# The last pair's second product as seven block products, its squares on ScalarE, and weight sums made later

## The chip, the cores and the metric
The kernel runs on one core of one Trainium2 chip (trn2). The time is the device time of the core in microseconds (us); the median of three runs before the change is 1382.69 us (1381.63 to 1384.86).

## What is computed
Attention without a softmax, normed per head, then two MLPs on 4608 tokens of width 512, all in f32:

```python
kv = einsum('bhsd,bhse->bhde', k, v); out = einsum('bhsd,bhde->bhse', q, kv)
x = out / sqrt(mean(out * out) + 1e-06) * g_norm           # 4608 x 512 after a transpose
r = maximum(x @ w_in, 0.0); x = (s * (r * r) + b) @ w_out  # first MLP, 2048 wide
h = maximum(maximum(x @ w1, x @ w2), x @ w3)               # second MLP, 768 wide
return h @ w_out2
```

## The kernel before, in words
Tokens lie in nine tiles of 512 columns. Each f32 product is three matmuls with rounded operands: high by high, high by low, low by high, so operands are split into two parts, the high one on ScalarE and the rest on VectorE (`hilo`, line 174).

**First MLP.** `h` has 16 chunks f of 128 rows, `y` four chunks j. Tiles 0 to 2 are multiplied plainly: for each f 12 matmuls for h, then relu, square times s (`squared`, line 437), plus b and split (`gate`, line 444), then 12 matmuls into four PSUM banks of y. Tiles 3 to 8 go in three pairs (ta, tb). The first product of a pair is made in eight turns q of seven block products (`h_steps`, line 658): 2x2 blocks with the two tiles as one side and two chunks f as the other, 6 matmuls each, 42 a turn where plain products would take 48. Their operands are sums of tokens (`tok_steps`, line 609) and sums of weights, 1792 KB a turn (`wp_dr`). A turn yields four blocks: chunks 2q and 2q+1 of each tile. Those of ta are gated at once, and the second product of ta runs beside the next turn (`y_mm`, line 469, 24 matmuls as fill). Those of tb go to DRAM (`g_dr`); after the eight turns the class `Second` (line 1402) reloads them one by one, gates each two chunks ahead and runs tb's second product, 192 matmuls.

**Second MLP.** Five groups of tokens (`SUPERS`, the first is tiles 1 and 2). In each, nine units `v1` (line 724) of seven block products, 42 matmuls a unit, with maxima between the three weights, then `Output` (line 798), again seven block products over three chunks. Units take weight sums of 1792 KB from DRAM (`wc_dr`), the output three such tiles (`wo_dr`).

**Weight preparation.** The class `Ahead` (line 512) holds a list of steps, each a load and a make: `pair_op` (sums for the pairs), `plain_op` (an f64 weight chunk to f32, stored), `combine` (four differences and sums of 256 columns, a split of 768 and one of 1024 columns, a 1792 KB store). `beside_of` spreads such steps and token operands over the matmuls counted by `tick`; from the third pair on they may be moved forward freely, before that they stand behind the last main instruction (`in_order`). Order within an engine is set at compile time by a scheduler from program order and dependences; every engine runs its queue in order, and all DMAs named here are issued by the SP queue.

**Buffers.** Gates: two, and one more (`gp`, `gS`), each high and low. Weight tiles of 1792 KB: two (`wa`), a third in the second MLP (`wb`). PSUM: four banks y, two h, one x, one more; in the second MLP four o, one each of a, b, x, d.

Of the kernel before, what the change touches and what calls it, by code (L numbers as in the profile page):

```python
# [8 lines left out]

# [61 lines left out]
def fused_kernel(ctx, tc, qt, kv, kvr, g_norm, w_in, w_out, s, b, w1, w2, w3, w_out2, out):  # L71
# [55 lines left out]
    g_sb, sb_sb, rsb = cst[:, 0:1], cst[:, 1:3], cst[:, 3:4]  # L127
    kvbd2 = ap1.tile([P, NP, 2, P], F32R, tag="kvbd", name="kvbd")
# [13 lines left out]
    wo_dr = [dram.tile([P, 2, 7, HW], F32, name=f"wo_dr{c}") for c in range(KM // 2)]  # L142
# [297 lines left out]

    turn = [0]
    w2p = {}

    def gate(r):
# [5 lines left out]
        nc.scalar.activation(out=gh, in_=r, func=ACTF.Identity, bias=sb_sb[:, 1:2])  # L450
        nc.vector.scalar_tensor_tensor(out=gl, in0=r, scalar=sb_sb[:, 1:2], in1=gh.bitcast(F32), op0=ALU.add, op1=ALU.subtract)  # L451
# [27 lines left out]
    def y_out(t, o, n, j, st, acc):  # L479
        y = yt[t, o][j][:, :n]  # L480
        if acc:
            nc.vector.tensor_tensor(out=st, in0=st, in1=y, op=ALU.add)
        elif j % 2:
            nc.scalar.activation(out=st, in_=y, func=ACTF.Copy)
        else:
            nc.vector.tensor_copy(st, y)
        store(y_dr[t][:, j, o:o + n], st)
# [66 lines left out]

    def combine(srcs, tile_of, dst):

        def blocks(t):
            return t.bitcast(F32).rearrange("p (n c) -> p n c", c=HW)
# [10 lines left out]
        return load, maker(got, blocks, tile_of, dst)  # L569

    def maker(got, blocks, tile_of, dst):

        def make():
# [9 lines left out]
            hilo(tgt[:, 0, 0:3], tgt[:, 1, 0:3], raw[:, 1:4])  # L583
            hilo(tgt[:, 0, 3:7], tgt[:, 1, 3:7], com)
            store(dst, tgt.bitcast(F32), 18)
# [72 lines left out]
    def h_steps(w, T, tb, q, gates):  # L658
# [3 lines left out]
        fa, fb = 2 * q, 2 * q + 1  # L662
# [10 lines left out]

        def keep(f, r):
            store(g_dr[tb][f], r)
# [15 lines left out]
        def p2():  # L691
# [3 lines left out]
            squared(r, a)  # L695
            gates[fa] = gate(r)

        def p4():
            d, r = got.pop("d"), fpool("r")
            prod(w, T, d, A22, "t4", False, False, end)  # L700
            nc.vector.tensor_tensor(out=r, in0=d, in1=got.pop("u2"), op=ALU.add)
            squared(r, r)
            gates[fb] = gate(r)

        def p5():
            x, r = got.pop("x"), fpool("r")
            prod(w, T, x, S1, "t1", False, False, end)
            got["b"] = copy(h_bank("b"), x)
            nc.vector.tensor_tensor(out=r, in0=x, in1=got.pop("p7"), op=ALU.add)
            squared(r, r)  # L710
            keep(fb, r)

        def p3():
            b, r = got.pop("b"), fpool("r")
            prod(w, T, b, S4, "b22", False, False, end)
            squared(r, b)
            keep(fa, r)
# [658 lines left out]
    direct = {}  # L1376
# [284 lines left out]
```

## Time and profile before
| | us |
|---|---|
| median of three runs | 1382.69 |
| profiled execution, device time | 1380.73 |
| its span, first to last instruction | 1378.9 |
| TensorE busy | 1363.6 |
| VectorE busy | 967.8 |
| ScalarE busy | 735.6 |

The span is cut into stages by the matmuls of the trace: the first pair's first product from 327.5 us, its stored half from about 463; the second pair from about 510, its stored half from about 645; the third pair from 688.0, its stored half from about 808; the second MLP from 853.5. PE is TensorE, DVE VectorE, ACT ScalarE, SP the queue that issues DMAs. Busy times of one engine overlap at the ends of instructions, and busy TensorE is modelled.

### The profile page before, as it was taken

The numbers are of one execution on the slowest core, as the hardware profiler recorded it, in microseconds if no ns is written. First come the engines' busy times: TensorE is split into PE (matmuls) and PEld (weight loads), VectorE is DVE, ScalarE is ACT, GpSimd is POOL, SyncE is SP. The second block draws the span as 40 slices with busy tenths as digits, with TensorE's granted clock in tenths as the row PEclk, the third lists the DMA queues.
The fourth block names the chain that finished last, engine by engine and source line by source line (L and its number), as shares of the span: only waits on it lengthen the run. The fifth ranks groups of instructions, "written<-read, shape, count | busy, mean of one in ns | idle before, by whom it ended". The sixth has DMA issues, their size and how long they took to land.

```text
span 1378.9 us, 19476 instructions
## 1 busy us (share of the span) xinstructions
PE 1363.6 (99%) x6870; PEld 1129.6 (82%) x6870; DVE 967.8 (70%) x1768; ACT 735.6 (53%) x1420; POOL 11.0 (1%) x40
## 2 busy tenths in 40 slices
PE   8999999999999999999999999999999999999998
PEld 6878887888888888887878878888998888888886
DVE  8999866678877678777967676547674574666555
ACT  7975655566776546565555554334453452443332
POOL 1000000000000000000000000000000000000000
PEclk9999999999999999999999999999999999999999
DMA  8486544585666856779898899955864554563532
GB/s 307 141 260 210 190 138 138 183 273 198 236 241 253 315 182 212 271 243 300 296 354 298 300 323 373 395 187 167 323 219 170 211 186 153 195 240 115 178 143 62
DMA packets 144584, 316.39 MB, mean 229 GB/s; under 512 B 62438, under 2 KB 82406, under 8 KB 133734
## 3 DMA queue, kind: packets, MB, share of 16 engines
q1 hardware_dynamic: 144480, 315.15, 65.9%
q8 instruction: 54, 0.88, 0.3%
q14 instruction: 44, 0.36, 0.1%
q10 hardware_dynamic: 6, 0.00, 0.0%
HBM read 222.30 MB, written 92.80 MB: 229 GB/s over the span
## 4 chain that ended last, share of the span: by engine, by line
PE 82%; DVE 8%; DMA 5%; issue 2%; ACT 2%; SPq 0%; POOL 0%; DVEq 0%; ACTq 0%; POOLq 0%
PE x L465 18%; PE y L465 18%; PE d L465 12%; PE o L465 9%; PE a L465 6%; PE b L465 6%; PE h L423 5%; PE y L151 2%; PE h L151 2%; DVE tb L151 1%; PE ops L343 1%; PE kvps L321 1%; DMA gb<-g_dr 1%; DVE head L151 1%; DMA raw<-in_w_in 1%
## 5 line engine op out<-in xcount | busy, mean ns | idle before, releaser
L465 PE MATMUL y<-gh,w 128*128 128x512 f32 x976 | 319.0, 391 | 1.3 <-ACT gh L450 1.1
L465 PEld LDWEIGHTS y<-gh,w 128*128 128x128 f32 x976 | 182.9, 188 | 40.1 <-ACT gh L450 2.0
L465 PE MATMUL d<-t,wc 128*128 128x512 f32 (+1 forms) x828 | 199.4, 376 | 0.3 <-ACT p L734 0.3
L465 PE MATMUL x<-t,wc 128*128 128x512 f32 (+1 forms) x828 | 199.5, 376 | 0.1
L465 PE MATMUL y<-gl,w 128*128 128x512 f32 x488 | 191.1, 392 | 1.0 <-DVE gl L451 0.8
L465 PEld LDWEIGHTS d<-t,wc 128*128 128x128 f32 x828 | 148.7, 188 | 28.4 <-ACT p L734 0.5
L465 PEld LDWEIGHTS x<-t,wc 128*128 128x128 f32 x828 | 148.3, 188 | 28.0 <-ACT a L671 0.5
L739 DVE TENSOR_TENSOR c<-d,u 128x512 f32<-128x512 f32 (+1 forms) x45 | 28.7, 638 | 134.7 <-PE d L465 134.7
L439 DVE SCALAR_TENSOR_TENSOR r<-r,cst 128x512 f32<-128x512 f32 x107 | 80.0, 749 | 47.3 <-ACT r L438 46.4
L465 PEld LDWEIGHTS y<-gl,w 128*128 128x128 f32 x488 | 91.7, 188 | 20.2 <-DVE gl L451 2.7
L465 PE MATMUL a<-b,wc 128*128 128x512 f32 (+1 forms) x414 | 100.1, 376 | 0.0
L465 PE MATMUL x<-b,wc 128*128 128x512 f32 (+1 forms) x414 | 99.9, 376 | 0.0
L465 PE MATMUL b<-b,wc 128*128 128x512 f32 (+1 forms) x414 | 99.5, 376 | 0.0
L465 PEld LDWEIGHTS b<-b,wc 128*128 128x128 f32 x414 | 74.4, 188 | 14.3 <-ACT b L671 0.4
L465 PEld LDWEIGHTS x<-b,wc 128*128 128x128 f32 x414 | 74.2, 188 | 14.0 <-issue 0.4
L465 PEld LDWEIGHTS a<-b,wc 128*128 128x128 f32 x414 | 74.2, 188 | 13.8
L465 PE MATMUL o<-t,wq 128*128 128x512 f32 (+1 forms) x354 | 75.5, 369 | 0.0
L734 ACT ACTIVATE a<-x 128x512 f32<-128x512 f32 (+1 forms) x45 | 24.3, 539 | 92.9 <-PE x L465 92.9
L151 PE MATMUL h<-xh,w 128*128 128x512 f32 (+1 forms) x216 | 72.0, 377 | 0.0
L465 PEld LDWEIGHTS o<-t,wq 128*128 128x128 f32 x354 | 62.4, 188 | 11.2
L734 ACT ACTIVATE b<-x 128x512 f32<-128x512 f32 (+1 forms) x45 | 24.3, 539 | 81.2 <-PE x L465 81.2
L151 PE MATMUL y<-gh,w 128*128 128x512 f32 (+1 forms) x200 | 65.2, 371 | 1.1 <-ACT st L151 1.1
(165 smaller groups left out, 2371.9 us busy)
## 6 DMA issues: line engine op xcount, KB each, us to landing
wc<-wc_dr SPq DMA_DIRECT2D x45, 1792.0 KB, 7.4
wc<-wp_dr SPq DMA_DIRECT2D x16, 1792.0 KB, 8.4
kv<-in_kv SPq DMA_DIRECT2D x32, 512.0 KB, 5.9
wc_dr<-hl SPq DMA_DIRECT2D x9, 1792.0 KB, 9.2
gb<-g_dr SPq DMA_DIRECT2D x62, 256.0 KB, 4.7
wp_dr<-wc SPq DMA_DIRECT2D x8, 1792.0 KB, 7.5
g_dr<-r SPq DMA_DIRECT2D x51, 256.0 KB, 2.6
y_dr<-st SPq DMA_DIRECT2D x48, 256.0 KB, 3.3
```

The lines of the kernel that those rows point to most:

```text
L151: tail[eng] = call(*args, **kw).ins
L321: nc.tensor.matmul(pb[d, i * D:(i + 1) * D], lhsT=t[:, 0, d], rhs=t[:, 1, d], start=(c == 0), stop=(c == NC))
L343: nc.tensor.matmul(pb, lhsT=l, rhs=r, start=(i == 0), stop=(i == 2))
L423: nc.tensor.matmul(h[:, :n], lhsT=w[:, z, kk, :], rhs=x[:, kk, o:o + n], start=(i == 0), stop=(i == 3 * KD - 1))
L439: main["dve"] = nc.vector.scalar_tensor_tensor(out=r, in0=r, scalar=sb_sb[:, 0:1], in1=r, op0=ALU.mult, op1=ALU.mult).ins
L465: ins = nc.tensor.matmul(*args, **kw)
L734: main["act"] = nc.scalar.activation(out=out, in_=pb, func=ACTF.Copy).ins
L739: main["dve"] = nc.vector.tensor_tensor(out=o, in0=pb, in1=t, op=ALU.add).ins
```

## The change
Three parts.

1. For the last pair (tiles 7, 8) the class `Blocks` takes the place of `y_mm` and `Second`. The second product is also made in seven block products, for each of 8 chunk pairs q, with 2 output parts of 128 rows and 3 matmuls each. Two of the seven (b11, t3) run beside the next turn of the first product; the other five in a run of 40 blocks behind it, each with a gate or split of its own. Results of the first product stay in the memory of used-up weights instead of DRAM. The weights for the blocks are made from `w_out` by `block_op`, one step for each q, among the preparations of the first two pairs (8 steps), go to DRAM (`ws_dr`, `wh_dr`), and come back in chunks of 1792 KB.
2. In all pairs s times the square of the relu is made on ScalarE as the square of root(|s|) times it, and the sum and relu in front of it by one custom VectorE instruction; the sign of s is put on b and on the results of the second product. `roots` makes root and sign once.
3. The sums of the second MLP's units 3 to 8 and two of the three output weights are no longer made in the last pair but in the first group, one step behind each of units 0 to 7, into the tiles in which they are used.

```diff
+    root, sign, bias, tmp = cst[:, 4:5], cst[:, 5:6], cst[:, 6:7], cst[:, 7:9]
...
+    def roots():
+        a, e = tmp[:, 0:1], tmp[:, 1:2]
+        s_, b_ = sb_sb[:, 0:1], sb_sb[:, 1:2]
+        nc.scalar.activation(out=a, in_=s_, func=ACTF.Abs)
...
+        nc.scalar.activation(out=root, in_=a, func=ACTF.Abs_reciprocal_sqrt)
...
+    def rooted(out, src, relu):
+        if relu:
+            nc.scalar.activation(out=out, in_=src, func=ACTF.Relu)
+        main["act"] = nc.scalar.activation(out=out, in_=out if relu else src, func=ACTF.Square, scale=root).ins
+
+    def relu_sum(out, bank, t):
+        main["dve"] = nc.vector._custom_dve(TENSOR_ADD_SAT, out=out, in0=bank, in1=t, s0=3.4028235e38, s1=0.0).ins
...
+    def scaled(st, y, by_act, signed=True):
+        if by_act:
+            nc.scalar.activation(out=st, in_=y, func=ACTF.Copy, **({"scale": sign} if signed else {}))
+        elif signed:
+            nc.vector.tensor_scalar(out=st, in0=y, scalar1=sign, scalar2=None, op0=ALU.mult)
...
-            squared(r, a)
-            gates[fa] = gate(r)
+            rooted(r, a, True)
+            sink(0, 0, r)
...
-            nc.vector.tensor_tensor(out=r, in0=d, in1=got.pop("u2"), op=ALU.add)
-            squared(r, r)
-            gates[fb] = gate(r)
+            relu_sum(r, d, got.pop("u2"))
+            rooted(r, r, False)
+            sink(1, 0, r)
...
+    def block_op(q):
...
+            for i, w in enumerate((fa, fb)):
+                hi, lo = (w[:, z].bitcast(F32).rearrange("p (n c) -> p n c", c=HW) for z in range(2))
+                nc.vector.tensor_tensor(out=raw[:, 2 * i:2 * i + 2], in0=hi, in1=lo, op=ALU.add)
...
+            tt(0, raw[:, 1], raw[:, 3], ALU.add)
+            tt(1, com[:, 0], raw[:, 0], ALU.subtract)
+            tt(2, raw[:, 2], com[:, 1], ALU.subtract)
+            tt(3, raw[:, 0], raw[:, 1], ALU.subtract)
...
+                hilo(hi, lo.bitcast(F32R), lo)
+                for k in range(2):
+                    store(to[2 * i + k][:, 0], hi[:, k].bitcast(F32))
+                    store(to[2 * i + k][:, 1], lo[:, k])
...
-    prep.todo += conv[:16]
+    parts = [block_op(q) for q in range(QF)]
+    for q in range(QF):
+        prep.todo += [parts[q], conv[q]]
...
+    prep.todo += [*conv[QF:], *com[:3], outs[2]]
+    inside = Ahead()
+    inside.todo += [*com[3:], *outs[:2]]
...
+    class Blocks:
...
+        def sink(self, q):
...
+            def sink(i, j, x):
+                r[i, j] = x
+                if (i, j) == (0, 0):
+                    self.op["b11", q] = gate(x, bias)
+                elif (i, j) == (0, 1):
+                    t3 = fpool("t3")
+                    sub(t3, r["b22", q], x)
+                    self.op["t3", q] = gate(t3, add=False)
+                    sub(r["t1", q], x, r.pop((0, 0)))
+                    sub(r["t2", q], r["b22", q], r["t1", q])
...
+        def mul(self, bk, e, m, first=False):
...
+            for i, (z, x) in enumerate(((0, hi), (0, lo), (1, hi))):
+                tied_mm(self.bank[bk, m], lhsT=w[:, z, m * P:(m + 1) * P], rhs=x, start=first and i == 0, stop=i == 2, skip_group_check=True)
...
+        def run(self):
+            for k, e in enumerate(self.order):
...
+                if k % 7 == 0 and 0 < k < 35:
+                    if k < 28:
+                        self.fetch(k // 7 + 1)
...
+                self.ready(k + 3)
+                for m in range(2):
+                    self.mul({"t2": "x", "b21": "a", "t1": "x", "t4": "d", "b22": "b"}[nm], e, m)
+                    tick(3)
...
-            beside_of([prep.step] * 12, 0, V + U)
+            beside_of([prep.step] * 14, 0, V + U)
...
-            beside_of([prep.step] * (len(prep.todo) - prep.made), 0, V + U + 2 * U // 3)
+            beside_of([prep.step] * (len(prep.todo) - prep.made), 0, V + U // 2 + 60)
...
-            beside_of([prep.step] * 4, 0, U)
+            beside_of([prep.step] * 8, 0, U)
...
-        after.run()
+        (blk or after).run()
...
+            if i < NQ - 1:
+                inside.step()
...
+            if i == NQ - 2:
+                scr.close()
+                wq[KC - 1] = pool("wq2", 1, side="right").tile([P, 2, 7, HW], F32R, tag="wq", name="wq")
+                dma(out=wq[KC - 1].bitcast(F32), in_=wo_dr[KC - 1])
```

## Rows read from the trace of the kernel before
**Rows 1.** The page: span, and busy time, share and instructions of each engine.
```profile
span 1378.9 us, 19476 instructions
PE 1363.6 (99%) x6870; PEld 1129.6 (82%) x6870; DVE 967.8 (70%) x1768; ACT 735.6 (53%) x1420; POOL 11.0 (1%) x40
```
**Rows 2.** Windows: stretch, length, busy us (instructions) PE/PEld/DVE/ACT/POOL, clock, DMA share, GB/s.
```profile
327.50:463.00 135.50, 135.26 (x754) 110.80 (x753) 103.11 (x193) 96.54 (x200) 2.42 (x8) 1.00 0.64 231
463.00:512.00 49.00, 48.78 (x216) 39.92 (x215) 37.09 (x65) 23.47 (x39) 0.00 (x0) 1.00 0.76 252
644.80:688.00 43.20, 42.28 (x186) 34.58 (x185) 37.59 (x66) 23.00 (x35) 0.00 (x0) 1.00 0.91 311
688.00:853.56 165.56, 164.65 (x722) 134.50 (x720) 120.18 (x196) 89.94 (x140) 0.00 (x0) 1.00 0.90 328
853.56:942.00 88.44, 88.44 (x390) 73.23 (x391) 42.48 (x67) 31.86 (x54) 0.00 (x0) 1.00 0.73 280
```
**Rows 3.** The chain that ended last, in order of time: start us, us, what.
```profile
709.63 2.72 PE y L465 x12
...
724.59 2.72 PE y L465 x12
...
810.90 5.90 DMA gb<-g_dr
```
**Rows 4.** Groups on VectorE: line, operation, shapes, count, busy us, mean ns, idle before.
```profile
L439 DVE SCALAR_TENSOR_TENSOR r<-r,cst 128x512 f32<-128x512 f32 x107 | 80.0, 749 | 47.3 <-ACT r L438 46.4
L451 DVE SCALAR_TENSOR_TENSOR gl<-gb,cst,gh 128x512 fp32r<-128x512 f32 x62 | 46.3, 748 | 16.5 <-ACT gh L450 16.5
...
L192 DVE CUSTOM_DVE_ANT_0 raw<-tab 128x1024 uint16<-128x1024 uint16 x24 | 16.5, 688 | 0.3
L701 DVE TENSOR_TENSOR r<-d,u 128x512 f32<-128x512 f32 x24 | 16.5, 687 | 0.2
...
L577 DVE TENSOR_TENSOR G<-F 128x256 f32<-128x256 f32 x40 | 15.9, 419 | 0.8 <-DMA F<-wf_dr 0.6
L176 DVE TENSOR_TENSOR hl<-G,hl 128x1024 fp32r<-128x1024 f32 x12 | 14.7, 1225 | 1.6 <-ACT hl L175 1.6
...
L176 DVE TENSOR_TENSOR hl<-F,hl 128x768 fp32r<-128x768 f32 x12 | 11.5, 956 | 9.9 <-ACT hl L175 9.9
```
**Rows 5.** Timeline of VectorE, second half of the second pair: start us, us, instruction.
```profile
670.40 0.75 DVE L451 SCALAR_TENSOR_TENSOR gl<-gb,cst,gh 128x512 fp32r<-128x512 f32 x1
671.06 0.69 DVE L631 TENSOR_TENSOR y<-y,y 128x512 f32<-128x512 f32 x1
671.66 0.69 DVE L176 TENSOR_TENSOR t<-y,t 128x512 fp32r<-128x512 f32 x1
```
**Rows 6.** Groups on ScalarE, columns as in rows 4.
```profile
L450 ACT ACTIVATE gh<-gb,cst 128x512 fp32r<-128x512 f32 x62 | 44.5, 720 | 32.6 <-DMA gb<-g_dr 12.4 <-PE y L465 10.7 <-ACT t L175 3.0
...
L438 ACT ACTIVATE r<-r 128x512 f32<-128x512 f32 x48 | 30.1, 628 | 15.2 <-DVE r L701 12.8 <-DVE r L709 2.2
```
**Rows 7.** DMA of 690 to 855 us (issues: KB each, us to landing); one issue's time.
```profile
DMA packets 18983, 54.25 MB, mean 329 GB/s; under 512 B 5857, under 2 KB 7393, under 8 KB 16797
...
wc<-wp_dr SPq DMA_DIRECT2D x6, 1792.0 KB, 8.5
...
wc<-wc_dr SPq DMA_DIRECT2D x2, 1792.0 KB, 15.0
...
699.69 0.32 SPq L157 DMA_DIRECT2D wc<-wp_dr  x1
```
**Rows 8.** DMA issues of 1050 to 1378 us.
```profile
wc<-wc_dr SPq DMA_DIRECT2D x24, 1792.0 KB, 7.3
```
**Rows 9.** Groups on VectorE from 853.56 to 942 us, columns as in rows 4.
```profile
L739 DVE TENSOR_TENSOR c<-d,u 128x512 f32<-128x512 f32 x9 | 6.2, 692 | 34.4 <-PE d L465 34.4
```
**Rows 10.** Waits of TensorE from 325 to 970 us: in total, times, longest.
```profile
PE y L465 <- ACT gh L450: 1.1, 2, 0.9
PE y L465 <- DVE gl L451: 0.8, 2, 0.6
```

More of the change, by code (lines that the diff above doesn't have):

```diff
@@ L141, in fused_kernel @@
     wc_dr = [dram.tile([P, 2, 7, HW], F32, name=f"wc_dr{i}") for i in range(NQ)]
-    wo_dr = [dram.tile([P, 2, 7, HW], F32, name=f"wo_dr{c}") for c in range(KM // 2)]
+    wo_dr = {c: dram.tile([P, 2, 7, HW], F32, name=f"wo_dr{c}") for c in (KM // 2 - 1,)}
+    BLOCK_Y = {len(PAIRS) - 1}
+    ws_dr = dram.tile([5 * QF, P, 2, HW], F32, name="ws_dr")
+    wh_dr = [dram.tile([P, 2, 2, HW], F32, name=f"wh_dr{q}") for q in range(QF)]
     opening = [True]
@@ L567, in load, with maker @@
                 dma(out=o, in_=src.rearrange("p (n c) -> p n c", c=HW))
-        return load, maker(got, blocks, tile_of, dst)
-    def maker(got, blocks, tile_of, dst):
+        return load, maker(got, tile_of, dst)
+    def maker(got, tile_of, dst):
         def make():
@@ L1420, in ready @@
                 if f not in self.gates:
-                    self.gates[f] = gate(self.rs.pop(f))
+                    self.gates[f] = gate(self.rs.pop(f), bias if self.t >= EDGE else None)
                 self.split += 1
@@ L1498, in fused_kernel @@
             w2p["p2"] = pool("prep2", 2, st=mlp1)
-            beside_of([prep.step] * (len(prep.todo) - prep.made), 0, V + U + 2 * U // 3)
-        after = Second(tb, list(range(KF)), {})
+            beside_of([prep.step] * (len(prep.todo) - prep.made), 0, V + U // 2 + 60)
+        if blk:
+            w2p["hw"] = pool("hw", 3, st=mlp1)
+            blk.load(0)
+        else:
+            after = Second(tb, list(range(KF)), {})
         for q in range(QF):
@@ L1516, in fused_kernel @@
                 step()
-                if q == QF - 1 and k == 0:
+                if end and k == 0 and not blk:
                     after.fetch(3)
                 tick(ONE // 2)
-        after.ready(1)
-        for f in (KF - 2, KF - 1):
-            for j in range(KD):
-                y_mm(ta, 0, TW, f, j, gates[f], False, f == KF - 1)
-                if f == KF - 1:
-                    y_out(ta, 0, TW, j, fpool("st"), False)
-                tick(3)
-            if f == KF - 2:
-                after.ready(2)
-        del yt[ta, 0]
+            if blk and not end:
+                blk.load(q + 1)
+        if blk:
+            blk.fetch(1)
+            for fn in fill + blk.beside(QF - 1)[:2]:
+                fn()
+                tick(3)
+            blk.copy("x", "a")
+            blk.ready(1)
+            for fn in blk.beside(QF - 1)[2:]:
+                fn()
+                tick(3)
+            blk.p7 = blk.kept("d")
+        else:
+            after.ready(1)
+            for f in (KF - 2, KF - 1):
+                for j in range(KD):
+                    y_mm(ta, 0, TW, f, j, gates[f], False, f == KF - 1)
+                    if f == KF - 1:
+                        y_out(ta, 0, TW, j, fpool("st"), False)
+                    tick(3)
+                if f == KF - 2:
+                    after.ready(2)
+            del yt[ta, 0]
         nxt = x_of(s + 1) if s + 1 < len(PAIRS) else y_of(0)
```

232 lines of the change are left out of this document (182 added, 50 removed).

## The prediction
> **What bounds the kernel now.** The page first: TensorE is busy for 99% of the span, VectorE for 70%, ScalarE for 53% [rows 1]. Modelled ends of matmuls can hide small gaps, so I counted instead. In the chain, one turn of the last pair's loop (42 matmuls of the first product, 24 of the second) begins at 709.63 and the next at 724.59 us: 14.96 us for 66, which is 0.2267 us for each 128x512 matmul [rows 3]. The windows then say where this pace is lost. The first group of the second MLP keeps it: 390 matmuls in 88.44 us [rows 2]. The last pair needs 720 x 0.2267 = 163.2 us and takes 165.56, so it loses 2.3 us [rows 2]; the chain shows one place, the reload of a stored gate, 5.90 us from 810.90 on [rows 3]. TensorE's recorded waits between 325 and 970 us are small, two of 1.1 us and two of 0.8 us in all, on the gate's two steps [rows 10]. The clock granted is 1.00 in all these stretches, the 2.4 GHz level [rows 2]. So the kernel is bound by the number of matmuls times a fixed pace, and a change gains what it removes from that number and loses what it makes TensorE wait.
>
> **Part 1, the block products.** The second product of tiles 7 and 8 has 2 x 16 x 4 x 3 = 384 matmuls now; seven products of 8 chunks, 2 output parts and 3 terms are 336. 48 go, all of one form: 48 x 0.2267 = **10.9 us** less, straight off the path. The first product keeps its 336. The Trainium skill (page "TensorE: Matmul & The Clock Gate", section "Back-to-back issue gap") gives about 131 ns for each matmul of 512 columns in a sustained stream; by that the 48 would be worth 6.3 us and the time 4.6 us longer than by my sum, an estimate from the page. The trace doesn't agree: it has 0.2267 in both stages and nothing closer, so the row decides and the page's case gets no chance of its own.
>
> In the turns of the first product, 54 matmuls or 12.2 us each now, the longest new chain is that of t3: relu, square, difference, split on both engines, about 3.2 us by these prices, against 6.8 us (30 matmuls) until its first use. I put 0 there; in the last turn, where the use comes after 18 matmuls, 4.1 us, the same.
>
> The 16 stores and 16 reloads of gates go from this pair, and with them the wait at 810.90. I take back half of the 2.3 us, **1.2 us**, between 0 and 2.3, since other late gates may stay.
>
> What replaces them has a tighter beat. Today a gate (ScalarE 0.72, VectorE 0.75 us [rows 4, 6]) feeds 12 matmuls, 2.72 us. In the new run of 40 blocks it feeds 6, 1.36 us. Gates have three buffers, so the gate of block k+2 can begin only when block k-1 is over: 2.72 us for a chain of 0.72 + 0.75 = 1.47. That leaves 1.25 us for queueing.
> VectorE's load there, at its back-to-back spacing of 0.66 (scalar form) and 0.60 us (plain) [rows 5]: 24 gates 15.8, 16 splits 9.6, 8 differences for t4 4.8, six evacuations 4, and the token operands of the second MLP, 22 operations, 13.2: 47.4 us of 240 x 0.2267 = 54.4 us, 87%. If two weight preparations (next part's price) still lie there it is over 100%. The stretch of 644.8 to 688 us ran at 37.59 of 43.20, 87%, and lost 0.9 us against its busy count [rows 2], with twice the slack for each gate.
> The weights of the blocks come in five chunks of 1792 KB; the third to fifth can be asked for only when a chunk has been used up, 42 matmuls or 9.5 us before they are needed. Under this pair's DMA load (329 GB/s) such loads landed in 8.5 us in the median, and the two of the second MLP's weights in 15.0; in the later, emptier stretch in 7.3 [rows 7, 8]. The new pair moves about 50 MB (8 weight pairs, 14 MB of block weights, the rest of the preparation) in 152 us, the same rate. So each of three chunks waits between 0 and 5.5 us; 8.5 is nearest, the same tile from the same queue in this pair, so I take 0 to 1 each. By the fit in the Trainium skill (page "DMA: Bandwidth & Descriptors", section "Anatomy of one DMA"), 2.0 us plus the bytes at 436 GB/s, a chunk would land in 6.2 us, an estimate from the page, with nothing to wait for; the rows are slower than that.
> Together I take **3.0 us** of new waiting in this run, bounds 0 and 16.
>
> **Part 2, squares on ScalarE.** In each of 24 turns four scalar-form operations of 0.75 us leave VectorE [rows 4]: 72 us in all. ScalarE gets two more of 0.63 us in a turn [rows 6], 30 us in all. Neither is on the path: VectorE was waiting for ScalarE in that very place, 46.4 us in all [rows 4]. ScalarE stood at 96.5 of 135.5 us in the first pair's first product [rows 2]; 16 x 0.63 makes it 106.6, 79%. The copies out of PSUM that TensorE needs have at least one product and two fills, 2.7 us, between them and their use, so I put 0, bounds -1 and +2. The fused add-and-relu is a custom operation the trace doesn't show with these operands; below it is the plain addition's 0.687 us, and the custom form in the trace takes 0.688 for the same bytes [rows 4]; above, the scalar form's 0.75. I take 0.69: nothing changes. The root of s, ten small operations once, in a chain over two queues in front of tile 2: between 0 and 2.5 us, **0.2** taken, since two PSUM buffers stand before TensorE. The sign in the evacuations replaces a copy from PSUM by a scale: nothing.
>
> **Part 3, block weights made ahead.** Eight new preparations, each at back-to-back spacing two additions 1.2, four of 256 columns 4 x 0.42 = 1.7, two splits 1.2: 4.1 us of VectorE, 1.3 of ScalarE and 11 stores on the DMA queue, 3.5 us of it at 0.32 each [rows 7], where nothing urgent but the next gate's reload stands behind them, asked for three gates ahead. Four of them, with four conversions that were there, go into the first pair's second half. VectorE was busy there 37.09 of 49.00 us [rows 2]; with 16.4 it is 53.5, over the stage. The work may slip into the next pair, which has 24 us freed by part 2, and no one waits for it soon; but it stands ahead of later gates, whose slack is two gates, 5.4 us. I take **0.8 us**, bounds 0 and 4.5 (the excess). The other four lie in the second pair, covered by its freed 24 us.
>
> **Part 4, weight sums inside the second MLP's first group.** Eight makes of 4 x 0.42 + 0.95 + 1.22 = 3.9 us [rows 4] leave the last pair, 31 us of VectorE, which is what makes room for part 1. They land in a group with VectorE busy 42.48 of 88.44 us [rows 2], so 73.5, 83%. Its idle time there lies in one place, before the sum c<-d,u: 34.4 us in 9, 3.8 each [rows 9], just a make. What a late make delays is the sum c22, which must clear bank x before the next unit: about 1.4 us of slack after c21. The stores of the sums (6 of 1792 KB) replace as many loads. The last output weight is loaded only after the eighth make has let its memory go, some 15 us (66 matmuls) before its first use, for 4 us of make and 8.5 to 12 us of landing. I take **1.2 us** for all of this, bounds 0 and 8.
>
> **Sum** against the profiled execution (1380.73 us, span 1378.9): -10.9 - 1.2 + 3.0 + 0.2 + 0.8 + 1.2 = -6.9. The median of the three runs, 1382.69, lies 1.96 above that execution; so 1382.7 - 6.9 = **1375.8 us**. A measurement of this kernel can tell 0.2%, 2.8 us, from no change: faster is under 1379.9, slower over 1385.5.
>
> **Rivals.**
> 1. *Everything is hidden.* The old waits go and no new one comes: -10.9 - 2.3 = -13.2, so 1369.5. For it: the first group kept the pace exactly, and VectorE sheds 72 us. Against: the gate's beat halves. Up to 1372 I give it 0.16.
> 2. *The gain is given back.* Chunk loads land late, at 12 us instead of 8.5 (3 x 2.5 = 7.5), and the first group waits some 2 us: about 1382, no change. For it: the 15.0 us landings, DMA at 329 GB/s. Against: no weight load made TensorE wait in the last pair of before. 0.14.
> 3. *Slower: the gates of the block run.* With three buffers a block takes (1.36 + 1.47 + w)/3 us, w being the time a gate queues behind other operations on the two engines. From w = 1.25 on TensorE waits; at 2.75, two foreign operations of 0.6 to 0.7 us ahead of it on each engine, a block takes 1.86, 0.5 more. Over the 28 blocks beside which token operands are made that is 14 us, and with nothing else lost -10.9 + 14 = +3.1: 1385.8, more with the other waits. It decides from w = 2.75 in most of these blocks. For it: VectorE at 87%, and gates in before stood behind such operations. Against: where operations are spaced evenly one foreign one at a time is the rule. 0.13.
>
> **How the numbers follow.** The forecast, the 48 matmuls gone and some 2 to 9 us of new waits, 1372 to 1379.9, has 0.57. Faster: 0.57 + 0.16 = 0.73; same: 0.14; slower: 0.13. The range goes from 1369.5, rival 1, to 1385.0, through rival 2; above it lies most of rival 3, and below it next to nothing.
>
> **What would show it.** TensorE's count 48 lower, and the last pair's stretch near 672 x 0.2267 = 152.3 us plus the waits. In the block run: ScalarE's gate waiting for TensorE's release (good) or TensorE for the gate (rival 3); a weight load of a block before which TensorE is idle (rival 2). In the first group: the idle time before c<-d,u shrunk from 3.8 us to little, with 88.4 us or more for 390 matmuls. In the first pair's second half VectorE near 100%. ScalarE up by some 55 us (30 squares, 10 splits of weights, 16 for 24 more gates) and VectorE about level (-72, then +33 for preparations, +16 for gates, +19 for differences). I am wrong if the pace itself changes, if the first two pairs take more than 2 us longer than now, or if the block run loses more than 8 us.

## The result and the profile after

The changed kernel takes 1401.98 us (median of four runs, 1400.74 to 1403.82) against 1382.47 for the kernel before (four runs): a ratio of 1.0139, interval 1.0122 to 1.0157. It is slower by 19.5 us where 1375.8 was forecast, and it lies outside the range given. The profiled execution took 1402.37 us, 21.6 more than the one of before (1380.73).

Its page, the lines that answer to [rows 1]:
```profile
span 1400.6 us, 19638 instructions
PE 1366.1 (98%) x6822; PEld 1124.3 (80%) x6822; DVE 971.0 (69%) x1802; ACT 793.8 (57%) x1516; POOL 11.0 (1%) x40
```
TensorE has 48 matmuls less, VectorE is level (+3), ScalarE has 58 us more: the work is what the prediction counted. So the loss is waiting. Its windows, cut at the same matmuls as [rows 2] (length; busy us PE, PEld, DVE, ACT, POOL; clock; DMA share; GB/s):
```profile
336.36:474.90 138.54, 136.60 (x754) 111.83 (x752) 85.11 (x169) 106.06 (x217) 2.41 (x8) 0.99 0.64 223
474.90:536.20 61.30, 57.80 (x245) 46.07 (x244) 48.91 (x93) 31.80 (x58) 0.00 (x0) 0.97 0.74 239
669.27:713.73 44.46, 43.95 (x193) 36.01 (x193) 36.52 (x64) 22.09 (x36) 0.00 (x0) 1.00 0.85 270
713.73:875.22 161.49, 156.69 (x674) 124.60 (x673) 113.47 (x186) 110.11 (x175) 0.00 (x0) 1.00 0.85 292
875.22:963.66 88.44, 88.44 (x392) 73.26 (x391) 69.71 (x115) 44.71 (x70) 0.00 (x0) 1.00 0.74 260
```
Against [rows 2]: the first pair's product 138.5 instead of 135.5 us, its second half 61.3 instead of 49.0, the second pair's half 44.5 instead of 43.2, the last pair 161.5 instead of 165.6, the first group 88.44 as before. And the first pair begins 8.9 us later, a stretch for which the prediction had no term but the 0.2 us of the roots.

All later comparisons use one table, read from the trace of each run: the first matmul `x<-b,wc` of the pairs' turns cuts the time, and each column is what a run loses against before in that stretch. "Opening": up to the first pair (327.37 us before). "Turn 0" of the first pair (11.98). "Turns": 1 to 7 (103.41). "Half": turn 7 to the second pair's turn 1, where the second half of the first pair lies (79.56). "Second pair": to the last pair's turn 1 (177.18). "Last pair": to the second MLP (154.04). The time of before next to these runs was 1382.07 to 1384.37. The compiler sets the order of TensorE anew in each run, so a column also holds matmuls that moved across a cut. Counted at 0.2267 us for 512 columns these are at most 1.5 us, but for three runs: in e4 some 4 us moved from the second pair into the half, in e13 some 3 and in e16 some 4 us from the half into the turns.

| run | us | opening | turn 0 | turns | half | second pair | last pair |
|---|---|---|---|---|---|---|---|
| after | 1402.37 | +8.9 | +3.4 | -0.3 | +12.3 | +1.4 | -4.0 |
| e1_pin_copies | 1407.44 | +2.3 | +1.2 | -0.3 | +17.4 | +9.1 | -3.3 |
| e2_pin_roots | 1403.64 | +10.5 | +1.6 | -0.3 | +13.5 | +1.9 | -4.2 |
| e3_pool_queue | 1407.73 | +7.4 | +3.2 | -0.3 | +6.7 | +13.4 | -3.9 |
| e4_steps_moved | 1407.65 | +10.2 | +1.5 | -0.3 | +3.7 | +16.0 | -4.7 |
| e5_no_prep | 1383.51 | +3.7 | +1.4 | -0.3 | -1.0 | +2.9 | -4.9 |
| e6_make_no_store | 1386.05 | +2.0 | +3.5 | -0.4 | +0.6 | +3.6 | -4.0 |
| e7_store_no_make | 1392.46 | +2.1 | +1.4 | -0.4 | +4.1 | +9.3 | -5.2 |
| e8_no_blocks | 1391.64 | +4.6 | +3.4 | -0.4 | -0.4 | +2.5 | -0.7 |
| e9_one_store | 1397.76 | +6.7 | -0.2 | -0.4 | +11.7 | +1.0 | -3.2 |
| e10_late | 1405.11 | +2.2 | +0.9 | -0.3 | +13.3 | +11.4 | -3.2 |
| e11_mended | 1393.98 | +2.0 | -0.5 | -0.3 | +12.3 | +3.9 | -4.2 |
| e12_no_blocks_one_store | 1385.06 | +3.4 | -0.5 | -0.3 | -1.0 | +1.8 | +0.2 |
| e13_in_turns | 1408.76 | +5.0 | -0.4 | +11.4 | +6.6 | +10.3 | -4.8 |
| e14_unlinked | 1407.17 | +2.9 | +1.3 | -0.3 | +15.6 | +10.4 | -3.5 |
| e15_low_in_f | 1409.76 | +2.8 | +0.5 | -0.3 | +18.1 | +11.8 | -3.8 |
| e16_in_turns_f | 1404.87 | +3.2 | -0.4 | +13.2 | +0.8 | +11.4 | -4.0 |
| e17_few_stores | 1397.55 | +2.3 | +3.2 | -0.3 | +12.1 | +2.5 | -3.4 |
| e18_tiny_stores | 1400.18 | +2.2 | +1.2 | -0.3 | +13.9 | +5.1 | -3.4 |

Single runs; the opening alone varies by some 2 us between executions (its 80th matmul began at 13.2 us in before and at 13.3 to 15.4 in e5, e6 and e8), so differences under 2 us are not read.

### The profile page after: what moved, and what is told of

It reads as the page before. It is cut to its first block, busy times and chain, and to the rows that moved or that the text cites. A ratio compares the mean times of both kernels' runs of the same rounds, so it can differ in the third digit from the quotient of the medians.

```text
span 1400.6 us, 19638 instructions
## 1 busy us (share of the span) xinstructions
PE 1366.1 (98%) x6822; PEld 1124.3 (80%) x6822; DVE 971.0 (69%) x1802; ACT 793.8 (57%) x1516; POOL 11.0 (1%) x40
## 4 chain that ended last, share of the span: by engine, by line
PE 68%; DVE 12%; DMA 11%; ACT 4%; issue 3%; SPq 1%; ACTq 0%; DVEq 0%
PE x L496 18%; PE d L496 12%; PE o L496 9%; PE y L496 8%; PE b L496 7%; PE a L496 6%; PE h L428 4%; DMA wf_dr<-raw 2%; DMA raw<-in_w_out 2%; DMA gb<-g_dr 2%; DMA raw<-in_w 2%; DVE tb L156 1%; PE y L156 1%; PE h L156 1%; DMA raw<-in_w_in 1%
## 5 line engine op out<-in xcount | busy, mean ns | idle before, releaser
L496 PE MATMUL y<-gh,w 128*128 128x512 f32 x720 | 237.5, 392 | 2.5 <-ACT gh L481 1.7
L496 PEld LDWEIGHTS y<-gh,w 128*128 128x128 f32 x720 | 135.1, 188 | 30.7 <-ACT gh L481 2.7
L496 PE MATMUL y<-gl,w 128*128 128x512 f32 x360 | 141.3, 393 | 0.4 <-DVE gl L482 0.4
L496 PEld LDWEIGHTS x<-b,wc 128*128 128x128 f32 x414 | 74.7, 189 | 15.6 <-ACT b L180 1.5
L496 PEld LDWEIGHTS a<-b,wc 128*128 128x128 f32 x414 | 75.2, 190 | 14.3
L496 PEld LDWEIGHTS y<-gl,w 128*128 128x128 f32 x360 | 68.0, 189 | 13.9 <-DVE gl L482 1.2
L428 PE MATMUL h<-xh,w 128*128 128x512 f32 x192 | 64.1, 392 | 0.1
```

Of the source, the lines that this page charges most:

```text
L428: nc.tensor.matmul(h[:, :n], lhsT=w[:, z, kk, :], rhs=x[:, kk, o:o + n], start=(i == 0), stop=(i == 3 * KD - 1))
L496: ins = nc.tensor.matmul(*args, **kw)
```

## The experiments

In the expectations, theory Q says that stores in SP's queue hold up the loads behind them (at first: because they wait there for their data), L that VectorE's new work stands in front of gates and evacuations, R that the block run or the squares cost, S that one store cut in two does.

**The opening: copies that float (e1, e2).** SP's timeline of after, in the opening (start us, us, instruction):
```profile
86.96 0.52 SPq L162 DMA_DIRECT2D ws_dr<-w  x1
87.83 0.33 SPq L156 DMA_DIRECT2D raw<-in_w_in  x1
...
96.88 0.33 SPq L156 DMA_DIRECT2D raw<-in_w_in  x1
```
Three of a step's 11 stores copy halves of resident weights. They depend on nothing but those weights, so the scheduler moved all 24 forward to where each weight is made (31 to 182 us, some 400 us ahead of their steps), into a queue that runs in order: a copy waits there for its weight (three times from 84 to 200 us, 9.7 us in all), and the loads of raw weights stand behind it. Before had these two loads at 84.69 and 91.44. e1 pins every copy behind the DMA that stands before it in the program; e2 keeps the roots where they are written.

```diff
...
-                store(dst, src.bitcast(F32))
+                store(dst, src.bitcast(F32), pin=True)
```


> The 24 stores of plain weight halves (three for each chunk pair) may no longer float ahead of their place in the program; they stand behind the store before them on the SP queue. Theory Q (a store that waits holds up the loads behind it on the SP queue): of the 8.8 us that are lost before the first pair, the 7.0 us between 160 and 177 us of the trace's matmuls number 200 to 960 come back, the first pair starts at about 329.5 us instead of 336.2, the time is about 1395 us; from there on the stages take as long as in the changed kernel, within 1 us. Theory P (the opening is late for another reason: the root's operations, other addresses in DRAM): less than 1.5 us come back, the time stays over 1400 us.

> The ten operations of the root stand behind the last square of the opening instead of floating into it. If they cost what the first 1.8 us of delay suggest (0.6 us at matmul 40, 1.8 at matmul 280), the first pair starts 1 to 1.8 us earlier, at about 334.5 to 335.2 us, and the time is about 1400.2 us. If that delay comes from the weight stores, which begin at the same place, the first pair starts at 336.2 us as before, within 0.4, and the time stays at about 1402 us.

e1 gives back 6.6 of the opening's 8.9 us; e2 gives nothing. So the copies are the opening's cost. What stays, 2.0 to 5.0 us in the runs with pinned or no copies, is partly the start-up variation and isn't settled. But e1 as a whole is slower, 1407.44 where about 1395 was expected: the same copies, now in their steps, cost 5 us in the half and 8 in the second pair.

**Turn 0: one store cut in two (e8, e9, e12).** The change to `maker` lets each prepared weight pair be stored in two pieces. SP's timeline of after before the first pair:
```profile
321.09 5.67 SPq L162 DMA_DIRECT2D wp_dr<-wc  x2
326.80 2.99 SPq L162 DMA_DIRECT2D y<-x_dr  x3
```
and the same place in e9, with one store:
```profile
318.63 3.62 SPq L162 DMA_DIRECT2D y<-x_dr  x3
323.73 0.32 SPq L162 DMA_DIRECT2D wp_dr<-wc  x1
```
In after the two pieces hold the queue for 5.67 us (4.5 of them waiting for VectorE's split), and three token loads stand behind. TensorE then waits for ScalarE, late with the token operands, in the first turn:
```profile
341.20 1.03 PE L496 MATMUL x<-t,wc 128*128 128x512 f32 x3 [1.94 <-ACT a L709]
```

```diff
-                if dst is not None:
+                if dst is not None and len(tgt) == 2:
                     store(dst[:, :, n], t.bitcast(F32), 18)
+            if len(tgt) == 3:
+                store(dst, tgt[2].bitcast(F32), 18)
...
```


> The change with one thing put back: each prepared pair of weights of the first product is stored in one piece again, after both of its splits, instead of in two pieces of three and four blocks. Theory S: the two pieces are one more store that waits at the head of SP's queue in front of the last token loads of the first pair; so its first turn takes 12 to 13 us (11.98 before, 15.36 after), and the time falls by 2 to 4 us to about 1399. If the first turn's loss comes from the squares or the roots: it stays at 14 us or more.

e8 leaves out the block products; e12 is e8 with this one store.

```diff
-    BLOCK_Y = {len(PAIRS) - 1}
+    BLOCK_Y = set()
...
```


> The change without its first part: the last pair's second product in the old form with 384 matmuls, no preparation of block weights; squares on ScalarE and the sums inside the first group stay. If the block run is worth what its trace shows (48 matmuls of 0.2267 us less some 7 us of new waits): 3 to 6 us above the run without preparation, so about 1386 if that has 1382. If squares and sums are free or a gain: 1378 to 1383, at or below the kernel before.

> Squares on ScalarE and sums inside the first group without the block products (1391.64), and with the one store put back. Theory S: the first turn of the first pair falls from 15.35 to 12 or 13 us and the time to about 1388. With what is left of the roots in the opening, still 2 to 5 us above the kernel before. If squares alone cost: no change.

Turn 0 goes from +3.4 to -0.2 in e9 and from +3.4 to -0.5 in e12; in each run with the one store it is -0.5 to -0.2, in those without +0.5 to +3.5. So the second piece is the cost of turn 0. e12, squares and sums without block products, is 1385.06 next to 1383.30: no gain from freeing 72 us of VectorE work, no loss beyond the opening's rest.

**The half: making alone, storing alone, both (e5 to e7, e14).** Four runs form a square: no preparations, preparations without stores, stores without preparations, and both with the tie between them cut (the stores carry slices of resident weights).

```diff
-    for q in range(QF):
-        prep.todo += [parts[q], conv[q]]
+    prep.todo += conv[:QF]
...
```


> The eight preparations of block weights are left out altogether (their 88 stores, their VectorE and ScalarE work); the block run loads as many bytes, already written weights of the first product, so what it multiplies is not the block weights. Squares, sums inside the first group and the block run stay. If the preparation is the whole cost (Theories Q and L alike): the first pair begins within 3 us of 327.4 (now 336.2), the step from its turn 7 to the second pair's turn 1 is within 2 us of 79.6 (now 91.9), and the time falls to about 1382, between 1378 and 1386. If squares on ScalarE or the block run carry a good part (Theory R): over 1390.

```diff
-                for k in range(2):
-                    store(to[2 * i + k][:, 0], hi[:, k].bitcast(F32))
-                    store(to[2 * i + k][:, 1], lo[:, k])
...
```


> The preparations are computed where they stand, but none of their 88 stores is issued; the block run reads as in the run without preparation, so its weights are not the block weights. Theory Q (stores that wait at the head of SP's queue and hold up the loads behind them): within 3 us of the run without preparation, and the step from turn 7 to the second pair's turn 1 under 83 us. Theory L (VectorE and ScalarE work in front of the gates and evacuations): that step stays over 87 us, and the time is 7 us or more above the run without preparation.

> The counterpart: the 88 stores are issued in their places, each pinned behind the DMA before it, but they carry slices of the resident weights, which have long been there; nothing is computed, so the block weights are wrong. If it is the waiting of the stores for their data that holds the queue (Theory Q): within 4 us of the run without preparation, the step under 83 us. If it is the mere number of the stores on that queue (0.4 to 0.5 us each): 4 us or more of loss in each of the stages where they stand, 8 us or more in all. Theory L: like the run without preparation.

```diff
...
-                    store(to[2 * i + k][:, 0], hi[:, k].bitcast(F32))
...
+                    store(to[2 * i + k][:, 0], fa[:, 0, :HW].bitcast(F32), pin=True)
...
```


> The run with pinned copies (1407.44) with the tie cut: all eight preparations are computed, and as many bytes are stored by as many stores in the same places, but these carry slices of resident weights that have long been there, so nothing waits for made data and no scratch buffer waits for a store; the block weights are wrong. If the tie is the cause: the step from turn 7 to the second pair's turn 1, 96.9 us there, falls to 83 to 86 (79.6 + 0.6 + 4), the second pair loses under 4 us, and the time is 1388 to 1395. If it is VectorE's load and DMA's load adding up: over 90, and over 1400.

Without preparations the time is 1383.51 next to 1382.65: they are the cost. In the half, making loses 0.6 us, storing 4.1, both 15.6; up to the last pair's turn 1 it is 4.2, 13.4 and 26.0, against 1.9 without either. And cutting the tie changes nothing (e14 1407.17, e1 1407.44): my theory that stores hold the queue because they wait for their data fell here, and e14 came out as expected for "VectorE's load and DMA's load adding up". What the four do shows in windows of 50 us, from 30 to 80 us after turn 7 of each. Before:
```profile
472.76:522.76 50.00, 49.78 (x220) 40.52 (x219) 36.45 (x61) 27.24 (x46) 0.00 (x0) 1.00 0.58 194
```
Making alone (e6):
```profile
477.84:527.84 50.00, 49.59 (x217) 40.01 (x216) 46.07 (x83) 30.37 (x51) 0.00 (x0) 1.00 0.60 200
```
Storing alone (e7):
```profile
475.94:525.94 50.00, 46.91 (x206) 37.86 (x205) 32.51 (x55) 23.66 (x41) 0.00 (x0) 1.00 0.92 307
```
Both, untied (e14):
```profile
476.68:526.68 50.00, 45.03 (x191) 35.96 (x189) 37.43 (x69) 24.96 (x47) 0.00 (x0) 0.97 0.84 274
```
With makes alone VectorE is busy 46.07 of 50 us and TensorE loses nearly nothing: it fits, barely. With stores alone VectorE gets 32.5 us done instead of 36.5, because what it needs comes late. With both it gets 37.4 done of the 46 it has: 8.6 us of work are pushed out of the window, and there is no slack to make them up.

Why things come late is seen in after, engine by engine. SP's queue, the eight stores of a step and what stands behind them:
```profile
483.91 2.84 SPq L162 DMA_DIRECT2D y<-x_dr  x3
486.79 0.43 SPq L162 DMA_DIRECT2D gb<-g_dr  x1
488.76 0.32 SPq L162 DMA_DIRECT2D ws_dr<-wh  x1
...
491.97 0.45 SPq L162 DMA_DIRECT2D wh_dr<-wh  x1
492.47 0.46 SPq L162 DMA_DIRECT2D wh_dr<-G  x1
492.97 0.45 SPq L162 DMA_DIRECT2D y<-x_dr  x1
493.47 1.41 SPq L162 DMA_DIRECT2D gb<-g_dr  x3
```
The same fourth token load in before:
```profile
474.37 1.11 SPq L157 DMA_DIRECT2D y<-x_dr  x1
```
ScalarE in after:
```profile
492.71 0.64 ACT L180 ACTIVATE t<-y 128x512 fp32r<-128x512 f32 x1 [0.61 <-DVE y L669]
498.12 0.63 ACT L180 ACTIVATE b<-y 128x512 fp32r<-128x512 f32 x1 [4.78 <-DMA y<-x_dr]
498.85 0.63 ACT L180 ACTIVATE t<-y 128x512 fp32r<-128x512 f32 x1
499.38 1.94 ACT L481 ACTIVATE gh<-gb,cst 128x512 fp32r<-128x512 f32 x3
```
VectorE:
```profile
498.12 0.69 DVE L669 TENSOR_TENSOR y<-y,y 128x512 f32<-128x512 f32 x1 [4.05 <-DMA y<-x_dr]
```
TensorE:
```profile
500.14 1.20 PE L496 MATMUL y<-gh,w 128*128 128x512 f32 x4 [1.69 <-ACT gh L481]
```
The fourth token load stands behind eight stores and is issued at 492.97, 38.3 us after turn 7 began where before has 31.6, and behind it the reloads of the next three gates, at 493.47. ScalarE reaches the split of these tokens at 493.3 and waits 4.78 us, with those gates queued behind it; VectorE waits 4.05 us, and TensorE waits for the gate. So a chain of in-order queues passes on the time of eight stores: SP, ScalarE, TensorE. In e14 the same load stands behind 11 stores and ScalarE waits 5.86 us for it.

This chain is one of several. TensorE's waits in after, 470 to 548 us (in total, times, longest):
```profile
PE mps L385 <- ACT sh L180: 3.0, 1, 3.0
PE y L496 <- ACT gh L481: 1.7, 1, 1.7
PE x L496 <- ACT b L180: 1.3, 1, 1.3
PE d L496 <- ACT p L709: 0.6, 1, 0.6
```
The second is the one just followed, and the third leads back to a token load (506.30) behind a store that had waited for its data until 505.93. Behind the other two, 3.6 of 6.6 us, stands ScalarE's own row: it came to sh at 538.18, after a split of block weights (536.12), a conversion (536.64) and two copies out of PSUM. Matmuls also ran slower after such waits: the mean granted clock was 0.93 from 498.00 to 546.52 us, between the levels of 2.4 and 1.2 GHz, which is some 3.4 us (0.07 of 48.5, an estimate).

**Queue time or bytes (e17, e18).** From e14: the same 1.84 MB a preparation in 4 stores, and 11 stores of 4 KB each. The block run loads other weights in both.

```diff
...
+            for k in range(4):
+                src = (fa, fb)[k % 2].rearrange("p z c -> p (z c)")[:, :DM * (2 if k < 3 else 1)]
...
```


> The unlinked run (1407.17: all eight preparations computed, stores of resident weights in their places) with the same bytes, 1.84 MB a preparation, in 4 stores instead of 11, with rows of 4 KB; block weights are not made available, the run loads other weights. Queue theory (each store takes SP 0.4 to 0.5 us, and loads behind it come later): 56 stores less are some 25 us of queue time, the loss from the first pair's turn 1 to the last pair, 25.8 us in the unlinked run, falls under 12, the time under 1395. Bytes theory (DMA engines full): it stays over 20, the time over 1402.

```diff
...
+            for k in range(11):
+                store(ws_dr[q][:, 8 * k:8 * k + 8], fa[:, 0, 8 * k:8 * k + 8].bitcast(F32), pin=True)
```


> The counterpart: 11 stores a preparation as in the unlinked run, of 8 columns each, so 1.84 MB become 45 KB. Queue theory: the loss stays over 18 us, the time over 1400. Bytes theory: under 8 us, the time near 1390, and the profile's DMA share in the half falls from some 0.9 to that of the run without stores. Both in part: between.

SP's timeline of e18 and then of e17, the same step:
```profile
477.43 0.43 SPq L162 DMA_DIRECT2D gb<-g_dr  x1
477.91 5.90 SPq L162 DMA_DIRECT2D ws_dr<-w  x11
483.85 0.43 SPq L162 DMA_DIRECT2D y<-x_dr  x1
```
```profile
479.59 0.43 SPq L162 DMA_DIRECT2D gb<-g_dr  x1
480.07 3.37 SPq L162 DMA_DIRECT2D ws_dr<-w  x4
483.48 1.11 SPq L162 DMA_DIRECT2D y<-x_dr  x1
```
Eleven stores of next to nothing hold the queue 0.54 us each, nearly as long as eleven of 128 and 256 KB do in e14 (11 in 7.6 us, 0.69 each); four large ones take 0.84 each. With hardly any bytes (DMA share 0.59 in that window, as in before) the half still loses 13.9 of 15.6 us. So bytes are not the half's cost. In the second pair both runs take back more: 10.4 falls to 2.5 with few stores and to 5.1 with tiny ones; there bytes and queue time seem both to count. From turn 1 to the last pair e18 loses 18.6 us, as the queue theory forecast (over 18). But it had asked for under 12 with few stores, and e17 loses 14.3, 12.1 of it in the half. In the half 7.6, 5.90 and 3.37 us of stores a step cost 15.6, 13.9 and 12.1 us. On a line through these, no queue time at all would still cost some 9 us (an estimate), and e6, without stores, loses 0.6. So queue time is a part of the half's loss, and the smaller one; that stores stand there at all does more, perhaps by the order of TensorE (see Open).

The Trainium skill (page "DMA: Bandwidth & Descriptors", section "Issuing engines are not separate DMA queues") says that the time to initiate a DMA "is usually small relative to the DMA itself". For one DMA the rows agree (0.54 us against a landing of 1.7 us or more); for a row of 11 ahead of a load on which two engines wait they don't: it takes 5.90 us, and e18 loses 13.9 us in the half with next to no bytes.

**Other queue, later, fewer, elsewhere (e3, e4, e10, e11, e13, e15, e16).** These came in between, each on a theory of its own.

e3 issues the 64 stores of made weights from POOL's queue:
```diff
...
+            if side:
+                nc.gpsimd.dma_start(out=o, in_=i)
...
```


> The 64 stores of split block weights are issued by the POOL queue instead of SP; the work of every engine stays. Theory Q (waiting stores on the SP queue hold up the reloads of gates and the tokens): the 12.3 us lost between the last turn of the first pair and the second turn of the second pair shrink to under 4 us, the time is about 1393 us. Theory L (VectorE has more to do in the first pair's second half than the half lasts, 53.5 us by my count): they stay above 9 us, the time is over 1398 us. In either case the opening stays as late as it is (first pair from about 336 us), since the 24 plain stores stay on SP.

The half falls from 12.3 to 6.7 us, between what the two theories asked for (under 4, over 9), and TensorE's 5.6 us of waits there are now for VectorE's low parts of gates. The waits of SP's queue in e3, 468 to 540 us (in total, times, longest), say what remained:
```profile
SPq L162 <- DMA wh_dr<-G: 14.6, 2, 11.7
```
Stores of low halves keep scratch buffers, and loads into these wait. The second pair lost 13.4, and the time rose to 1407.73.

e4 leaves four of the eight steps in the first half:
```diff
...
-            beside_of([prep.step] * 8, 0, U)
+            beside_of([prep.step] * 4, 0, U)
```


> Of the eight preparation steps in the first pair's second half four (two block weights, two conversions) move into the second pair. Theory L: VectorE's demand in the half falls from 53.5 to about 40 us of 43.5, under the stage; the 12.3 us fall to 1 to 3, the second pair gains less than 2, the time is about 1393 us. Theory Q: each of the two block weights that are left still holds the SP queue once, so about half stays, 5 to 7 us, and the time is about 1396 us.

The half falls to 3.7 us, no more than the matmuls that moved into it, and the second pair rises to 16.0, with the same 4 us taken out: the loss goes with the steps, and grows there (1407.65, where the two theories forecast 1393 and 1396).

e10 puts e1's stores 24 matmuls behind their step, e15 puts its low halves into other buffers:
```diff
...
-                    store(to[2 * i + k][:, 0], hi[:, k].bitcast(F32))
...
+                    store(to[2 * i + k][:, 0], hi[:, k].bitcast(F32), 24)
...
```


> The run with pinned copies again (1407.44), with one number changed: the 64 stores of made block weights are put into SP's queue 24 matmuls (5.4 us) after their step instead of 9 (2.0 us). Theory Q: they then find their data ready, and the step from turn 7 of the first pair to turn 1 of the second falls from 96.9 to under 90 us, the second pair's two jumps of 5 and 6 us to under 3 each; the time under 1397. If the number of stores or VectorE's load is what costs: no fall by more than 3 us. A middle way: the stores are late, the scratch buffers with the low halves stay taken longer, and conversions wait for them; then the halves gain and the turns don't.

```diff
...
-                hilo(hi, lo.bitcast(F32R), lo)
+                low = w2p["f"].tile([P, 2, HW], F32R, tag="f", name="wl")
+                hilo(hi, low, lo)
...
```


> The run with pinned copies (1407.44) with the low halves written into two buffers of the larger pool that already takes the high halves, so the scratch buffer is free as soon as VectorE is done, while the stores still wait on the queue for their data. If held scratch buffers are the larger part: the step falls from 96.9 to under 90 and the time by 7 us or more. If the waiting at the queue's head is: the step stays over 93, the time within 4 us.

Against e1's 17.4 in the half they show 13.3 and 18.1: later stores give back some 4 us there (and lose 2 in the second pair), other buffers nothing.

e11 mends all that was known then: one store for a pair, copies pinned, roots in place, 6 stores a step, later.
```diff
...
+                store(ws_dr[:, 4 * i:4 * i + 3:2, q, 0], hi.bitcast(F32), 24)
+            store(ws_dr[:, 0:7:2, q, 1], com, 24)
...
```


> The whole change with four things mended: one store for a prepared pair, block weights laid out so that a step has 6 stores instead of 11, those of made weights 24 matmuls after their step and the copies pinned, and the roots kept where they are written. By Theories Q and S: first pair from 327 to 330 us on, its first turn under 13 us, the first half (turn 7 to the second pair's turn 1) under 84 us (79.6 before, 91.9 after), the last pair as in the change (4 us less than before); together 1383 to 1389. If it is VectorE's load after all: the half stays over 88 us, the time over 1393.

It is the fastest whole version of the change, 1393.98, and takes back 6.8 us of the opening and turn 0; the half stays at 12.3 over before, 91.9 us in all, as the expectation had it "if it is VectorE's load after all" (over 88). e13 moves its preparations into the turns of the loop, e16 adds e15's buffers:
```diff
...
                 beside_of([prep.step], 3, 10)
+                beside_of([early.step], 30, 36)
...
```


> The mended version (1393.98) with six of the eight preparations moved from the first pair's second half and the second pair into turns 1 to 6 of the first pair's loop, one in each, and two into the second pair; the conversions stay where they were before the change. Place theory: the turns have VectorE at 71 of 114 us and DMA at 63%, so the half falls back to within 2 us of 79.6, the turns lose at most 0.5 us each, and the time is 1380 to 1386. If a preparation costs some 1.5 us wherever it stands: the half gains 12 and the turns lose 9, about 1390.

> The run with preparations in the first pair's turns, and the low halves in the larger pool too. If scratch buffers matter in the turns, where a pair's preparation runs beside each: 2 to 4 us less than that run; if not, the same within 1.5 us, or more if the larger pool runs short.

The place theory fell: without the matmuls that moved the turns lose 8.6 and 9.0 us, the half still 9.7 and 5.7, and the sum is worse. e16 is 3.9 us below e13, as forecast if scratch buffers matter, but 1.8 of these lie in the opening. TensorE's longest waits in the turns of e13 (347 to 459 us) are not for a load:
```profile
PE x L501 <- DVE r L471: 5.7, 3, 2.7
```
In turn 5 this sum and relu, at 416.61, stands on VectorE behind the additions and splits of a preparation, from 409.41 on. So a stage whose busy shares leave room (VectorE 71 of 114 us) still has none in the order of VectorE's queue.

**The last pair (e5 against e8).** The same kernel without preparations, with block products and without: -4.9 against -0.7. So the 48 matmuls, 10.9 us, are worth 4.2 us net. In time e8 lies 8.1 us above e5, not the 3 to 6 expected: turn 0 adds 2.0 and the opening 1.0. The waits of TensorE in after, 713 to 876 us (in total, times, longest), answer to [rows 10]:
```profile
PE b L496 <- ACT b L709: 1.3, 2, 0.9
PE d L496 <- DVE gl L181: 1.1, 3, 0.4
PE d L496 <- ACT gh L180: 0.8, 1, 0.8
PE x L496 <- ACT a L1661: 0.6, 1, 0.6
PE x L496 <- ACT gh L481: 0.6, 1, 0.6
PE x L496 <- DVE gl L482: 0.4, 1, 0.4
```
No weight load is among them (`wc<-ws_dr` landed in 8.3 us in the median). Counted by the spacing of matmuls against 0.2267 us, the turns lose 2.9 us and the block run 5.6, 3.4 of these in the blocks of t4.

No run is faster than before. e5 says why none of these can be by much: even with the preparations gone it ends 0.9 us behind; with its opening and turn 0 as in before (3.7 + 1.4) it would be at 1378.4, 2 to 4 us ahead (an estimate).

## Why the prediction was wrong

**Part 1.** The count is exact (6870 to 6822), and the pace holds. The step that is off is the term for new waits: 3.0 forecast in the block run, 5.6 measured; nothing forecast in the turns beyond the 1.1 left of the old waits, 2.9 measured. The last pair gains 4.0 us instead of 9.1. My fear, late chunks, did not come; the gates of rival 3 did, 3.4 us, a quarter of its price, in the blocks that have a difference in front of their split.

**Part 2.** Right: nothing gained, ScalarE +58 as forecast (55), and the roots cost nothing that e2 could give back.

**Part 3 is the step that failed.** I priced a preparation's 11 stores at 3.5 us of the queue "where nothing urgent but the next gate's reload stands behind them", and took 0.8 us, bounds 0 and 4.5. Measured: 12.3 in the half. Three things were wrong. The token loads of the next pair stand in the same queue, ScalarE and VectorE meet their operands ahead of gates, and the gates' reloads, asked for three gates ahead, come late by the same row of stores. The issue time of 0.32 us [rows 7] was that of a lone load; in a row a store takes 0.54 to 0.69. And VectorE's excess and the queue's were priced one by one, each by its own slack: alone they cost 0.6 and 4.1 us, together 15.6 in e14. That each used the slack on which the other's price rested fits this, but isn't shown apart from TensorE's order (see Open). The second pair, "covered by its freed 24 us", lost 1.4 us in after, and 9.1 in e1, where the copies stand in their steps.

**Stores that were not in the sum.** That copies without a producer may move past anything (8.9 us in the opening, 6.6 of them given back by e1), and that `maker` now stores each pair in two pieces (3.4 us in turn 0, all given back by e9): both could be read in the code, and neither had a term. With them go 10.0 of the 21.6 us.

**Part 4.** Right in mechanism, and 1.2 us too dear: the group keeps 88.44 us with VectorE at 69.71 (73.5 forecast). VectorE's idle time before c<-d,u, 34.4 us in [rows 9], has shrunk as foreseen:
```profile
L774 DVE TENSOR_TENSOR c<-d,u 128x512 f32<-128x512 f32 x9 | 6.2, 689 | 6.1 <-PE d L496 6.1
```

**The rivals.** That it would be slower had 0.13, for a mechanism in the last pair; the loss came before that pair. The sentence on what would make me wrong, "if the first two pairs take more than 2 us longer than now", is what happened: 16.8 us without the opening.

**Open.** The compiler also ordered TensorE differently: in after the next pair's first product is woven into the half from 43 us after turn 7 on, in before and in runs e3 to e6 it begins at 67.8 to 75. e7 and e14 both have the woven order and lose 4.1 and 15.6, so the order alone isn't the loss; what it adds wasn't tried. It is a strong rival to queue time: all ten runs that lose 11.7 us or more in the half have it, e17 and e18 among them, and none without it loses more than 6.7 there (9.7 in e13 without the moved matmuls). The stores bring it about, since e6 hasn't got it, so they stay the cause in either case; but making alone, 0.6 us in e6, was never measured in the woven order. So it is shown that preparations with stores cost the half its 12.3 us, and that bytes don't; how much goes through SP's queue, how much through ScalarE's and VectorE's row and how much through the order stays open.

## What to carry to other kernels

Count a new store by what stands behind it in its queue and by which engine meets that data first, not by its bytes alone; a store without a fresh producer needs a pin, or the scheduler may put it hundreds of microseconds ahead. When a change takes slack from two resources of one stage, price both together: here making and storing cost 0.6 and 4.1 us apart and 15.6 together. And run a version without the new preparation early: e5 told in one run that at best a few microseconds were to be had.

## What the runs showed of the hardware

A store of 4 KB held SP's queue nearly as long as larger ones: 0.54 us each in a row of 11, against 0.69 for eleven of 128 and 256 KB. TensorE's granted clock fell after some waits and not after others: in turn 0 of e8, windows of 4 us behind a wait of 1.96 us,
```profile
334.00:338.00 4.00, 2.04 (x7) 1.35 (x6) 3.11 (x6) 2.75 (x5) 0.00 (x0) 0.88 0.44 171
338.00:342.00 4.00, 4.00 (x15) 3.24 (x14) 0.00 (x0) 0.90 (x2) 0.00 (x0) 0.69 0.19 66
```
and the same place in e5, behind a wait of 1.56 us:
```profile
334.00:338.00 4.00, 2.44 (x11) 1.99 (x11) 1.74 (x3) 2.69 (x5) 0.00 (x0) 1.00 0.53 199
338.00:342.00 4.00, 4.00 (x20) 3.21 (x18) 1.36 (x2) 3.26 (x7) 0.00 (x0) 1.00 0.00 0
```
The first two clocks are means over the levels of 2.4 and 1.2 GHz, the last two the higher level throughout. In the second window e8 gets 15 matmuls done where e5 gets 20, and turn 0 loses 3.4 us instead of 1.4: a wait can cost more than its length.
